# Attention and two MLPs on one core: weight conversions in every second item of attention instead of every third, and the combined tokens' last step in two pieces

## The chip, the core and the metric

The kernel runs on one core of a Trainium2 chip. A core has a matrix engine (PE, with its weight loads listed apart as PEld), a vector engine (DVE), an activation engine (ACT), a general engine (POOL) and a queue engine (SP), and DMA engines that move data. Each engine works through its own list of instructions in order, and waits on semaphores for the others. The metric is the device time of one execution in microseconds (us); a smaller number is better.

## What is computed

The reference runs three blocks one after the other, in float32 outputs:

```python
x = attention(q, k, v, s)            # 2 batches, 8 heads, 576 positions, 64 per head; causal, with a decay bias
x = x.transpose(0, 2, 1, 3).reshape(1152, 512)
h = x @ w_in;  x = maximum(0.01 * h, h) @ w_out        # w_in 512 x 2048, w_out 2048 x 512
p = domain_probs / domain_probs.sum(-1)                # 1152 x 4
out = sum over e of p[:, e] * (maximum(x @ w1[e], 0) @ w2[e])   # 4 experts, 512 x 1024 x 512
```

The weights `w_in` and `w_out` arrive as 64-bit floats, and the chip turns them into 32-bit ones. Every matrix operand is used as a pair of a rounded value (hi) and the rest (lo), and a product is three matmuls: hi with hi, lo with hi, hi with lo.

## The kernel before

The 1152 tokens are cut into a first part of 512 (part 0) and a second of 640 (part 1, 2 x 320). The program has these stretches, in the order of the trace:

- **Attention for part 0** (to about 67 us), then **attention for part 1** (to about 200 us). An item is one tile of queries and one or two heads; eight units of five items make up part 1. In each item there are three places at which other work is woven in. Each item's own steps (scores, exponentials, transposes, values, a finish) are spread over the following items by `STEPS` (L781).
- **The first MLP on part 0** (`mlps(phases[0])`, called `main`) is woven into attention and goes on after it up to about 228 us. Its up products are `ps_u<-x,w`, its down products `ps_d<-ht,w` with 512 columns; ACT and DVE turn an up product into the pair `ht`, and DVE adds a down product to `y`.
- **The first MLP on part 1** (about 228 to 334 us), then **the four experts** (to the end). Up products here go over combined tokens and combined weights: 7 products in the place of 8 (`paired_up`, L392), `ps_u<-t,w`.

Weights of the first MLP come in 16 units of 128 x 1024 numbers. `supply()` (L139) converts them, one unit after the other. One unit is an ACT instruction (`raw<-r`), two TENSOR_SCALAR and two SCALAR_TENSOR_TENSOR on DVE (`raw<-raw`, `raw<-r,raw`), each followed by a `yield`; then `finished()` issues the store of the unit to memory (`w_f<-raw`, from ACT's queue) and the fetch of the next 64-bit unit but one (`r`, also ACT's queue). Where the unit is needed at once, `finished()` also splits it into its pair (`w<-raw` on ACT, `w<-raw,w` on DVE). Otherwise `late_splits()` (L118) loads it back from `w_f` over SP's queue once its store was issued, and splits it in two halves of 512. At most four split units are held ahead (`WB`), and four `raw` buffers (`RAW`) are shared by all of these.

After attention, `first_sevens()` (L213) loads the first two weights of the MLP on part 1 from `w_f` and combines them: POOL makes the sums (`sums<-raw`), ACT rounds (`w<-raw`, `w<-sums`), POOL subtracts (`w<-sums,w`). At the same time `paired_steps()` (L364) combines the tokens of part 1, for two halves k of the 512 features: DVE makes four sums (`sums<-x`), then ACT rounds (`t<-x`, `t<-sums`) and DVE subtracts (`t<-x,t`, `t<-sums,t`). It is called again for part 0 and part 1 before the experts, then from `y`.

The order of instructions on each engine is the order of the program to the end of the first MLP on part 0 (`fixed = True`); from L898 a scheduler chooses it, and only the DVE subtractions of `paired_steps` stay in their order among those kept. In the attention loop for part 1 (L866 to L875) `at_ % 3` is the place in the item (0, 1, 2) and `i` the item: `main` gets places 0 and 1, `late_splits` places 0 and 2, and `supply` places 0 and 2 and place 1 of every third item. After attention (L885 to L893) `main` goes on, and every second step of it takes a step of one of the others. When attention closes (L876, L881) its memory and its accumulator banks are given up, and new pools are opened over them.

Of the kernel before, what the change touches and what calls it, by code (L numbers as in the profile page):

```python
# [19 lines left out]
def attention_moe_moe2(ctx: ExitStack, tc: tile.TileContext, q, k, v, s, w_in, w_out, probs, w1, w2, out):  # L20
# [54 lines left out]
    def f32(ap):  # L75
        return ap.bitcast(F32)
# [287 lines left out]
    def paired_steps(s, of, pool):  # L364

        n = half[s]
        t = t7[s] = pool.tile([P, 2, 7, 2, n], F32R, tag=f"t7_{s}", name=f"t7_{s}")
        for k in range(2):
            b11, b12 = of[:, k, :n], of[:, k, n:]
            b21, b22 = of[:, 2 + k, :n], of[:, 2 + k, n:]  # L370
            sums = scratch.tile([P, 4 * 320], F32, tag="scratch", name="sums")[:, : 4 * n].rearrange("p (s t) -> p s t", s=4)
            def subtract(*args):
                tc.keep_in_program_order(nc.vector.tensor_tensor(*args, ALU.subtract))

            subtract(sums[:, 1], b12, b11)
            subtract(sums[:, 2], b22, sums[:, 1])
            yield
            subtract(sums[:, 3], b22, b12)
            subtract(sums[:, 0], b21, sums[:, 2])
            yield  # L380
            for i, j, x in ((0, 2, of[:, k::2, :n]), (2, 3, of[:, 2 + k : 3 + k, n:]), (3, 7, sums)):
                hi, lo = (t[:, l, i:j, k] for l in range(2))
                nc.scalar.copy(hi, x)
                subtract(lo, x, f32(hi))
                yield
# [179 lines left out]
    def idling(n):  # L565

        for _ in range(n):
            nc.tensor.matmul(nothing[:, :P], idle[:, :P], idle[:, :P], start=True, stop=True)
# [209 lines left out]
    ending = False  # L778
# [4 lines left out]
    def attention():  # L783

        nonlocal ending
        items, starts, n = [], {}, 0
        i, split = 0, iter(())
        while n < units or i < len(items) + 8:
            if n < units and i == len(items):
                u = Unit(n)  # L790
                starts[n] = i
                items += [(u, *of) for of in u.items]
                if n + 2 < units and not 0 <= n + 2 - 2 * NP < 2:
                    load_keys(n + 2)
                    if n + 2 < 2 * NP:
                        decay(n + 2, k_e[(n + 2) % 3])
                if n in (2 * NP - 4, 2 * NP - 2):
                    load_keys(n + 4 if n == 2 * NP - 4 else n + 3)
                n += 1
            if n < units - 1 and i == starts[n - 1] + 2:  # L800
                load_values(n + 1)
            if i == starts[n - 1] and 2 * NP <= n < units:
                split = split_keys(n)
            for step, lag in STEPS:
                if 0 <= i - lag < len(items):
                    u, *of = items[i - lag]
                    step(u, *of)
                if lag == 1:
                    next(split, None)
                if lag in (1, 3, 7):  # L810

                    late = i - 5 + (lag == 7)
                    ending = lag != 3 and 0 <= late < len(items) and items[late][1:] == items[late][0].items[-1]
                    yield i
            i += 1
# [9 lines left out]
    with ExitStack() as phase:  # L825
        x_t[0] = phase.enter_context(tc.tile_pool(name="x0pool", bufs=1)).tile([P, 2, KD, sizes[0]], F32R, name="x0")
        wpool = phase.enter_context(tc.tile_pool(name="wpool", bufs=4))
        r64p = phase.enter_context(tc.tile_pool(name="r64p", bufs=2))

        OPENED = (24, 25, 26, 27, 28, 29, 31, 33, 35)  # L830

        CONVERTING = (*range(5, 16), *range(17, 31, 2))
        side, units_of_w, late, opened = attention(), supply(), late_splits(), 0
        nothing = ps_mm.tile([P, 512], F32, tag="mm", name="nothing")
        with tc.tile_pool(name="early", bufs=1) as early:
            ones = pads(early)
            sums = cumulative()
            next(sums)
            main = mlps(phases[0])

            for at_ in range(3 * 64):
                i = next(side)
                if done == 2 * NP and at_ % 3 == 2:
                    break
                if at_ % 3 == 0 and i in (6, 8):
                    nc.scalar.copy(q_s[i // 2 - 3][D:DK, 1, :, :QC], ones[D:DK])
                if at_ % 3 == 1:
                    if i < 18:
                        idling(2 if i < 6 else 1)
                    elif opened < len(OPENED) and i >= OPENED[opened] and opened < 3 * (done // 2):  # L850
                        next(main)
                        opened += 1
                if at_ % 3 < 2 and i >= 31:
                    onto_held()
                if at_ % 3 == 2:
                    if i == 3:
                        fetch64(1)
                    if i in (3, 4, 5):
                        next(sums)
                    if i in CONVERTING or i >= 31:  # L860
                        next(units_of_w)
        hidden_pool(phase, 6)
        heading = False

        owed = 0
        for at_, i in enumerate(side):  # L866
            if at_ % 3 < 2:
                owed += WOVEN * KD / (2.0 * (40 - 6))
                while owed >= 1.0:
                    next(main)  # L870
                    owed -= 1.0
            if at_ % 3 != 1:
                next(late, None)
            if (at_ % 3 != 1 or i % 3 == 0) and not ending:
                next(units_of_w, None)  # L875
        attn.close()  # L876
        w7pool = ctx.enter_context(tc.tile_pool(name="w7pool", bufs=2, side="right"))
        scratch = ctx.enter_context(tc.tile_pool(name="scratch", bufs=2, side="right"))
        t7pool = ctx.enter_context(tc.tile_pool(name="t7pool", bufs=1, side="right"))
        tokens = paired_steps(1, x_t[1], t7pool)  # L880
        banks.close()  # L881
        ps_mm = ctx.enter_context(tc.tile_pool(name="ps_all", bufs=8, space=PSUM))

        sevens = first_sevens()
        for m, _ in enumerate(main):  # L885
            if m % 2 == 0:
                next(late, None)
            if m % 4 == 0:
                next(tokens, None)
            if m % 4 == 2:  # L890
                next(units_of_w, None)
            if m % 4 % 2 and m >= 4:
                next(sevens, None)  # L893
        for _ in sevens:
            pass
        for _ in tokens:
            pass
# [57 lines left out]
```

## Time and profile before

| | us |
|---|---|
| median of 3 executions | 720.54 (717.39 to 970.85) |
| the profiled execution | 717.48 |
| its span, first to last instruction | 715.70 |

Share of the span in which an engine was busy: PE 97%, PEld 88%, DVE 61%, ACT 44%, POOL 35%. The granted clock of PE has a mean of 0.998 of full speed. A busy share is an average over stretches of different kind, and matmuls are pipelined with modelled ends; so the rows to read are those of a stretch, with the idle time in square brackets ahead of an instruction and, behind the arrow, what ended that idle time.

### The profile page before, as it was taken

Reading aid. Unit: us, or ns where it says so; the run is one execution under the profiler, and the core shown is the slowest. Engines: PE = TensorE matmul, PEld = TensorE weight load, DVE = VectorE, ACT = ScalarE, POOL = GpSimd, SP = SyncE. Lnnn points to the kernel's source line nnn. Section 1 sums busy time; section 2 is a strip of 40 time slices with the busy share of each in tenths; the row PEclk is TensorE's granted clock in tenths of the full one; section 3 lists DMA queues with packets and bytes.
Section 4 is the critical chain, followed back from the end, with each engine's and each line's share of the span. In section 5 each row is a group of like instructions: output and inputs, shape, how many; then the busy total and the mean of one; then the engine's idle time right before and its main releaser. Section 6 shows DMA issues by size and latency. Waiting matters only on the chain.

```text
span 715.7 us, 11167 instructions
## 1 busy us (share of the span) xinstructions
PE 696.9 (97%) x4256; PEld 633.2 (88%) x4256; DVE 433.7 (61%) x867; ACT 315.1 (44%) x640; POOL 253.9 (35%) x232
## 2 busy tenths in 40 slices
PE   8899999999988999999999999999999999999998
PEld 8778888888877999999988989889899898898986
DVE  7778788897767657735943634435435454364452
ACT  5757977875644574624422413323223142141210
POOL 6000000000039787964382522804526137142200
PEclk9999999999999999999999999999999999999999
DMA  9877688746442321320211211102011011010002
GB/s 232 207 195 208 194 211 245 220 143 235 177 177 61 118 82 66 119 60 30 60 60 31 59 31 59 60 1 89 31 57 54 8 60 60 1 59 1 1 36 97
DMA packets 43124, 69.61 MB, mean 97 GB/s; under 512 B 5616, under 2 KB 24832, under 8 KB 43072
## 3 DMA queue, kind: packets, MB, share of 16 engines
q1 hardware_dynamic: 32544, 40.83, 20.0%
q10 hardware_dynamic: 9376, 25.73, 10.6%
q0 software_dynamic: 1152, 2.36, 1.9%
q8 instruction: 33, 0.54, 0.3%
q14 instruction: 19, 0.16, 0.1%
HBM read 58.06 MB, written 10.82 MB: 96 GB/s over the span
## 4 chain that ended last, share of the span: by engine, by line
PE 82%; DVE 7%; DMA 4%; ACT 2%; POOL 2%; issue 1%; SPq 0%; ACTq 0%; POOLq 0%; DVEq 0%
PE ps_d L43 39%; PE ps_u L43 34%; PE ps_o L43 4%; PE ps_sc L43 3%; PE ps_pt L43 2%; DVE raw L43 2%; DMA qe<-in_q_dram 1%; DVE t L43 1%; ACT w L43 1%; DVE z L43 1%; DMA vs<-in_v_dram 1%; DMA raw<-w_f 1%; DMA ke<-in_k_dram 1%; DVE w L43 1%; POOL sums L43 1%
## 5 line engine op out<-in xcount | busy, mean ns | idle before, releaser
L43 PE MATMUL ps_u<-t,w 128*128 128x320 f32 (+1 forms) x1680 | 236.5, 299 | 1.1 <-DVE t L43 1.1
L43 PEld LDWEIGHTS ps_u<-t,w 128*128 128x128 f32 x1680 | 233.0, 189 | 4.8 <-DVE t L43 1.4
L43 PE MATMUL ps_d<-w,ht 128*128 128x512 f32 (+1 forms) x876 | 203.4, 388 | 0.0
L43 PEld LDWEIGHTS ps_d<-w,ht 128*128 128x128 f32 x876 | 161.0, 188 | 31.5
L43 POOL TENSOR_TENSOR w<-raw,w 128x512 fp32r<-128x512 f32 (+2 forms) x72 | 108.0, 1522 | 218.9 <-ACT w L43 218.9
L43 ACT ACTIVATE ht<-ps_u 128x320 fp32r<-128x320 f32 (+2 forms) x176 | 74.4, 433 | 153.7 <-DVE ps_u L43 129.0
L43 PE MATMUL ps_d<-ht,w 128*128 128x320 f32 (+1 forms) x576 | 111.0, 343 | 4.7 <-DVE ht L43 2.8
L43 DVE SCALAR_TENSOR_TENSOR oacc<-ps_d,pn,oacc 128x512 f32<-128x512 f32 (+1 forms) x64 | 47.5, 742 | 104.0 <-PE ps_d L43 104.0
L43 ACT CAST w<-raw 128x512 fp32r<-128x512 f32 (+2 forms) x94 | 64.5, 722 | 87.4 <-PE ps_d L43 67.7
L43 PEld LDWEIGHTS ps_d<-ht,w 128*128 128x128 f32 x576 | 92.3, 190 | 12.0 <-DVE ht L43 3.2
L43 DVE SCALAR_TENSOR_TENSOR ht<-ps_u,ht 128x320 fp32r<-128x320 f32 (+1 forms) x128 | 56.3, 452 | 23.3 <-ACT ht L43 22.0
L43 DVE TENSOR_TENSOR ps_u<-ps_u,tmp 128x320 f32<-128x320 f32 (+1 forms) x120 | 56.2, 471 | 23.3 <-PE ps_u L43 21.7
L43 POOL TENSOR_TENSOR sums<-raw 128x256 f32<-128x256 f32 x48 | 38.4, 818 | 66.1 <-PE ps_d L43 64.6
L43 DVE TENSOR_TENSOR tmp<-ps_u,tmp 128x320 f32<-128x320 f32 (+1 forms) x80 | 36.8, 463 | 40.4 <-PE ps_u L43 39.4
L43 POOL TENSOR_TENSOR w<-sums,w 128x1024 fp32r<-128x1024 f32 x24 | 58.2, 2424 | 5.3 <-ACT w L43 5.3
L43 PEld LDWEIGHTS ps_o<-vs,pv 128*128 128x128 f32 x400 | 53.5, 191 | 6.8 <-issue 2.3
L43 PE MATMUL ps_u<-x,w 128*128 128x512 f32 x192 | 56.3, 410 | 0.9 <-DVE x L43 0.9
L43 PE MATMUL ps_o<-vs,pv 128*128 128x65 f32 (+1 forms) x400 | 53.3, 267 | 2.1 <-DVE xo L43 1.2
L43 POOL DMA_DIRECT2D kd<-in_k_dram x8 | 4.8, 603 | 127.3 <-PE ps_sc L43 67.0
L43 ACT ACTIVATE z<-z,mn 128x256 f32<-128x256 f32 (+4 forms) x72 | 42.4, 588 | 12.0 <-DVE mn L43 7.2
L43 DVE CUSTOM_DVE_ANT_0 z<-ps_sc,mask 128x256 f32<-128x256 f32 (+4 forms) x72 | 36.0, 501 | 12.5 <-PE ps_sc L43 9.7
L43 ACT COPY pv<-ps_pt 128x512 f32<-128x512 f32 (+3 forms) x80 | 33.2, 424 | 21.2 <-PE ps_pt L43 20.7
(78 smaller groups left out, 647.0 us busy)
## 6 DMA issues: line engine op xcount, KB each, us to landing
raw<-in_moe_w_dram SPq DMA_DIRECT2D x32, 512.0 KB
raw<-w_f SPq DMA_DIRECT2D x22, 512.0 KB
r<-in_moe_w_in_dram ACTq DMA_DIRECT2D x8, 1024.0 KB
w_f<-raw ACTq DMA_DIRECT2D x16, 512.0 KB
r<-in_moe_w_out_dram ACTq DMA_DIRECT2D x8, 1024.0 KB
kd<-in_k_dram POOLq DMA_DIRECT2D x8, 288.0 KB, 6.0
kr<-in_k_dram SPq DMA_DIRECT2D x8, 288.0 KB
vs<-in_v_dram SPq DMA_DIRECT2D x8, 256.0 KB
```

What stands on the lines that cost most here:

```text
L43: ins = call(*args, **kw)
```

## The change

Two lines are edited. In `paired_steps` the last step, over the four sums at once (slots 3 to 6 of the seven), is made in two pieces, of slots 3 and 4 and of slots 5 and 6; each has its ACT instruction, its DVE subtraction and its `yield`. In the attention loop for part 1, `supply` gets place 1 of every second item instead of every third.

```diff
@@ paired_steps
-            for i, j, x in ((0, 2, of[:, k::2, :n]), (2, 3, of[:, 2 + k : 3 + k, n:]), (3, 7, sums)):
+            for i, j, x in ((0, 2, of[:, k::2, :n]), (2, 3, of[:, 2 + k : 3 + k, n:]), (3, 5, sums[:, :2]), (5, 7, sums[:, 2:])):
                 hi, lo = (t[:, l, i:j, k] for l in range(2))
                 nc.scalar.copy(hi, x)
                 subtract(lo, x, f32(hi))
                 yield
@@ the attention loop
             if at_ % 3 != 1:
                 next(late, None)
-            if (at_ % 3 != 1 or i % 3 == 0) and not ending:
+            if (at_ % 3 != 1 or i % 2 == 0) and not ending:
                 next(units_of_w, None)
```

**DVE at the end of attention.** The names: `raw` is a unit under conversion (`raw_2285` is the last of the 16 before, `raw_2227` after), `xo` the last output of attention, `ht` a hidden tile, `w` a split weight, `y0` the sum of down products of part 0. Before:

```order
L43 TENSOR_TENSOR w_2294<-raw_2232,w_2294 128x512 x2
L43 TENSOR_SCALAR raw_2285<-raw_2285 128x1024
L43 TENSOR_SCALAR st_2319<-ps_o_2221 128x6
L43 RECIPROCAL st_2319<-st_2319 128x6
L43 TENSOR_TENSOR xo_2322<-ps_o_2221,st_2319 128x384
L43 TENSOR_SCALAR raw_2285<-raw_2285 128x1024
L43 TENSOR_TENSOR ht_2328<-ps_u_2300,ht_2328 128x512
L43 SCALAR_TENSOR_TENSOR raw_2285<-r64_2219,raw_2285 128x1024 x2
L43 TENSOR_TENSOR w_2341<-raw_2308,w_2341 128x512 x2
L43 TENSOR_TENSOR y0_1310<-ps_d_2333,y0_1310 128x512
```

The same place after the change:

```order
L43 SCALAR_TENSOR_TENSOR raw_2227<-r64_2136,raw_2227 128x1024 x2
L43 TENSOR_TENSOR ht_2308<-ps_u_2271,ht_2308 128x512
L43 TENSOR_TENSOR w_2312<-raw_2251,w_2312 128x512 x2
L43 TENSOR_SCALAR st_2335<-ps_o_2240 128x6
L43 RECIPROCAL st_2335<-st_2335 128x6
L43 TENSOR_TENSOR xo_2338<-ps_o_2240,st_2335 128x384
L43 TENSOR_TENSOR ht_2343<-ps_u_2319,ht_2343 128x512
L43 TENSOR_TENSOR w_2351<-raw_2317,w_2351 128x512 x2
L43 TENSOR_TENSOR y0_1317<-ps_d_2347,y0_1317 128x512
```

The four conversion instructions of the last unit no longer stand between `w`, `xo`, `ht` and `y0`: the last pair of them now stands ahead of the `ht` two places earlier, and the rest further up.

**DVE where the first combined tokens are made**, after attention (`t7_1` are the combined tokens of part 1, `sums` their sums for k = 0). Before:

```order
L43 TENSOR_TENSOR t7_1_2387<-x1_98,t7_1_2387 128x320
L43 TENSOR_TENSOR ht_2462<-ps_u_2437,ht_2462 128x512
L43 TENSOR_TENSOR t7_1_2387<-sums_2388,t7_1_2387 128x4x320
L43 TENSOR_TENSOR ht_2485<-ps_u_2466,ht_2485 128x512
L43 TENSOR_TENSOR sums_2496<-x1_98 128x320
```

After:

```order
L43 TENSOR_TENSOR t7_1_2399<-x1_98,t7_1_2399 128x320
L43 TENSOR_TENSOR ht_2474<-ps_u_2449,ht_2474 128x512
L43 TENSOR_TENSOR t7_1_2399<-sums_2400,t7_1_2399 128x2x320
L43 TENSOR_TENSOR ht_2497<-ps_u_2478,ht_2497 128x512
L43 TENSOR_TENSOR t7_1_2399<-sums_2400,t7_1_2399 128x2x320
L43 TENSOR_TENSOR y0_1317<-ps_d_2501,y0_1317 128x512
```

The second hidden tile (`ht_2485`, now `ht_2497`) stood behind all four slots and now stands between the two pieces. ACT's list has the same shape at this place: the second `ht` behind the first piece, the second piece behind the `ht`.

**SP's loads of stored weights**, over the whole program (each row 128 x 1024 numbers; other loads stand between the rows). Before, then after:

```order
L43 DMA raw<-w_f_73 128x1024
L43 DMA raw<-w_f_73 128x1024 x10
L43 DMA raw<-w_f_73 128x1024 x11
```

```order
L43 DMA raw<-w_f_73 128x1024
L43 DMA raw<-w_f_73 128x1024
L43 DMA raw<-w_f_73 128x1024
L43 DMA raw<-w_f_73 128x1024
L43 DMA raw<-w_f_73 128x1024 x10
L43 DMA raw<-w_f_73 128x1024 x11
```

There are 22 such loads before and 25 after; the three more are units that `late_splits` loads back, and they stand among the loads of attention's keys and values.

## Rows read from the trace of the kernel before

**Rows 1.** Waits of PE: waiting tile, releaser, us in total, times, longest.

```profile
PE ps_d L43 <- DVE ht L43: 2.8, 1, 2.8
PE ps_d L43 <- DVE y L43: 1.9, 1, 1.9
PE ps_u L43 <- DVE t L43: 1.1, 1, 1.1
```

**Rows 2.** Timeline of PE from 190 us: start, duration, instruction, count, [idle before].

```profile
196.21 3.68 PE L43 MATMUL ps_d<-ht,w 128*128 128x512 f32 x15
201.76 5.71 PE L43 MATMUL ps_d<-ht,w 128*128 128x512 f32 x24 [1.88 <-DVE y L43]
207.31 5.60 PE L43 MATMUL ps_u<-x,w 128*128 128x512 f32 x24
212.75 2.71 PE L43 MATMUL ps_d<-ht,w 128*128 128x512 f32 x11
218.25 10.29 PE L43 MATMUL ps_d<-ht,w 128*128 128x512 f32 x37 [2.79 <-DVE ht L43]
```

**Rows 3.** Windows: length, busy time by engine (count), PE's clock, DMA share, GB/s.

```profile
200.00:202.00 2.00, 0.24 (x1) 0.27 (x2) 1.97 (x6) 0.15 (x1) 0.00 (x0) 1.00 0.22 88
...
218.00:220.00 2.00, 1.75 (x4) 1.41 (x5) 1.97 (x4) 0.00 (x0) 1.92 (x3) 0.59 0.08 2
220.00:222.00 2.00, 2.00 (x6) 1.53 (x5) 1.58 (x4) 0.84 (x1) 2.00 (x3) 0.55 0.05 5
```

**Rows 4.** Timeline of DVE around the end of attention.

```profile
195.81 2.48 DVE L43 SCALAR_TENSOR_TENSOR raw<-r,raw 128x1024 uint32<-128x1024 uint32 x2
...
200.93 0.68 DVE L43 TENSOR_TENSOR y<-ps_d,y 128x512 f32<-128x512 f32 x1
...
207.51 0.69 DVE L43 TENSOR_TENSOR y<-ps_d,y 128x512 f32<-128x512 f32 x1 [1.24 <-PE ps_d L43]
...
214.23 3.37 DVE L43 TENSOR_TENSOR t<-sums,t 128x1280 fp32r<-128x1280 f32 x1 [2.15 <-ACT t L43]
217.52 0.68 DVE L43 TENSOR_TENSOR ht<-ps_u,ht 128x512 fp32r<-128x512 f32 x1
```

**Rows 5.** Timeline of ACT in the same stretch.

```profile
199.42 0.73 ACT L43 CAST t<-x 128x640 fp32r<-128x640 f32 x1
...
210.77 0.59 ACT L43 ACTIVATE ps_u<-ps_u 128x512 f32<-128x512 f32 x1
211.98 1.05 ACT L43 CAST w<-sums 128x1024 fp32r<-128x1024 f32 x1 [0.62 <-POOL sums L43]
212.94 1.26 ACT L43 CAST t<-sums 128x1280 fp32r<-128x1280 f32 x1
214.10 0.58 ACT L43 ACTIVATE ht<-ps_u 128x512 fp32r<-128x512 f32 x1
```

**Rows 6.** Timelines of POOL and of SP's queue in that stretch.

```profile
213.86 2.39 POOL L43 TENSOR_TENSOR w<-sums,w 128x1024 fp32r<-128x1024 f32 x1
...
201.08 1.74 SPq L43 DMA_DIRECT2D raw<-w_f  x4
```

**Rows 7.** Window over attention for part 1, columns as in rows 3.

```profile
60.00:200.00 140.00, 137.83 (x875) 120.89 (x873) 117.60 (x220) 102.00 (x188) 3.49 (x6) 1.00 0.66 197
```

**Rows 8.** DVE by line, 60 to 200 us: count | busy us, mean ns.

```profile
L43 DVE SCALAR_TENSOR_TENSOR raw<-r,raw 128x1024 uint32<-128x1024 uint32 x26 | 31.7, 1219 | 0.4
L43 DVE TENSOR_SCALAR raw<-raw 128x1024 f32<-128x1024 f32 (+1 forms) x26 | 17.9, 689 | 0.3
```

**Rows 9.** Timeline of DVE and POOL ahead of the experts.

```profile
338.12 1.48 DVE L43 TENSOR_TENSOR t<-sums,t 128x1280 fp32r<-128x1280 f32 x1
...
345.91 3.38 DVE L43 TENSOR_TENSOR t<-sums,t 128x1280 fp32r<-128x1280 f32 x1
...
345.54 6.02 POOL L43 TENSOR_TENSOR w<-raw,w 128x1024 fp32r<-128x1024 f32 x2 [15.26 <-ACT w L43]
```

**Rows 10.** DVE by shape, 335 to 352 us: count | busy us, mean ns.

```profile
L43 DVE TENSOR_TENSOR t<-y,t 128x640 fp32r<-128x640 f32 x2 | 1.6, 816 | 0.0
```

## Prediction

> **What bounds the kernel now.** The busy shares and the waits of PE come first. PE is busy 97% of the span (the table of the profile above), and nearly all that it waits for is in three lines: a hidden tile `ht` 2.8 us, a sum `y` 1.9 us and combined tokens `t` 1.1 us, once each [rows 1]. So the change can gain only at these three places, or lose by making PE wait where it does not now. The timeline of PE tells where the first two are: both just after attention, at 201.76 and 218.25 [rows 2]. The 24 products from 201.76 to 207.31 take 5.55 us, 0.231 us each; this pace gives what each place really costs, since a busy matmul's end is modelled.
>
> - First gap: 15 products from 196.21 would be over at 196.21 + 15 x 0.231 = 199.68; the next starts at 201.76 [rows 2]. Lost 2.08 us.
> - Second gap: 11 products from 212.75 end at 215.29; the next starts at 218.25 [rows 2]. Lost 2.96 us.
> - [...] The 37 products from 218.25 last 10.29 us less about 0.16 of overhang (5.71 - 5.55), that is 10.13; at the pace they need 8.55 [rows 2]. Lost 1.58 us.
>
> These are 6.62 us in all. In attention itself PE idles 140.00 - 137.83 = 2.17 us while DVE is busy 117.60 of 140.00 [rows 7]: PE sets the time there, and DVE, at 84%, is close behind.
>
> **Why the two gaps are there.** At the first, PE starts the first product in the reopened accumulators, and is released by the sum `y` that DVE begins at 200.93 [rows 4], over a second after its products were done. DVE was late: the last unit's two bit operations hold it from 195.81 for 2.48 us, and what follows in its list is late in turn [rows 4]. At the second, PE needs the rest of the hidden tile, made at 217.52. DVE had it behind the subtraction over four slots, 3.37 us from 214.23, which began when ACT's rounding of those slots (212.94, 1.26 us) was done; that in turn stood behind `w<-sums` at 211.98, which waited for POOL's sums [rows 4, 5]. POOL's sums wait for a load that SP issues at 201.08 with three others [rows 6], behind the store of the last unit.
>
> **The supply in every second item.** Attention for part 1 covers about 40 items, so place 1 comes some 20 times instead of 13: seven steps more, a little over one unit of six. The order agrees: the last unit's instructions leave the end of attention for a place two hidden tiles earlier.
>
> First gap. With the 2.48 us gone, and two TENSOR_SCALAR ahead of it, DVE is free when the last products are done. `y` then starts as at 207.51, 0.04 us behind the end of its products (201.76 + 5.71 = 207.47) [rows 2, 4], so at 196.21 + 3.68 + 0.04 = 199.93. It lasts 0.68, to 200.61; PE starts 0.15 later, as before (201.76 against 200.93 + 0.68), at 200.76. **Gain 1.00 us.** Bounds: 0 if another instruction is late there, 1.00 if none, since PE must wait for this sum anyway.
>
> Second gap, upstream. The last store no longer waits for bit operations that end at 198.3, so the loads queued behind it on SP and POOL's sums come earlier too, and ACT's `w<-sums` need not wait for POOL. This alone moves ACT only by the 0.62 us of its idle time [rows 5]; it counts together with the pieces, below.
>
> Cost in attention. One more unit lies there: two SCALAR_TENSOR_TENSOR of 1.219 us and two TENSOR_SCALAR of 0.689 us [rows 8], 3.82 us, and its split in two 512-wide subtractions, by the 0.68 us of the 512-wide `y` [rows 4] 1.36 us: 5.2 us of DVE in the 22.4 us that it is idle [rows 7]. DVE works in order; behind an inserted operation wait reads of scores and sums, and PE for these. Nothing if the idle time takes them, 5.2 us if all lies on the path. A gain cannot be ruled out: the units stand more evenly now, and at most the 2.17 us of idle time is to be had. PE loses 2.17 us while DVE is 84% busy; in proportion, 5.2 us more on 117.6 would cost 0.1 us, but waits grow faster than load when an engine fills up, so I take **0.5 us**.
>
> The three more loads of 0.5 MB, from 22 to 25, add 1.5 MB to 197 GB/s over 140 us (27.6 MB), at a DMA share of 0.66 [rows 7]. They stand on SP ahead of loads of keys and values, and each waits for its store; the loads behind them come some us later, but are wanted a unit or two later (17 us a unit: 140 us over some eight units). Nothing, and if a unit came too late, a few us once. A late split is in two halves of 512 and so costs an instruction more on ACT and DVE, 3 times, some tenths of a us off the path.
>
> **The last step in two pieces.** At the second gap the hidden tile now stands behind the first piece only, on ACT and DVE. All PE times move up by the 1.00 of the first gap. ACT: the second write of the first hidden tile starts at 210.77 - 1.00 = 209.77 and ends 0.59 later, at 210.36; `w<-sums` takes 1.05, to 211.41; the first piece, as wide as the 0.73 us row at 199.42, ends at about 212.1 [rows 5]. The second tile's products are over at 207.31 + 5.60 - 1.00 = 211.9, so ACT makes its `ht` from 212.1 (0.58) and the second write behind it (0.59), to 213.3. DVE: the first piece from 212.1. Its cost is not in the trace; the 640-wide subtraction alone is 0.816 us [rows 10], half of the 3.37 is 1.69 us [rows 4]. POOL works at this place (2.39 us from 213.86) [rows 6], and it will have its rounding done about as early as DVE, so I take 1.69: to 213.8. The rest of `ht` takes 0.68, to 214.5, and PE follows 0.05 later (217.52 + 0.68 against 218.25). PE wants it at 215.29 - 1.00 = 214.29. Lost about 0.2 to 0.4 where 2.96 were: **gain 2.55 us**. Bounds: 2.96; and 0.69 if ACT and DVE keep their old times, only 1.69 us is saved and PE waits 1.00 longer.
>
> Here the trace shows four slots at 1.48 us while POOL is idle and at 3.38 us while POOL works [rows 9]. [...] At 0.82 us a piece `ht` would start at 213.3, the gap would be gone and the sum 0.4 us lower.
>
> The clock. With a gap of 0.4 us, far under the 2.08 us behind which the clock stayed up, it should not fall: **gain 1.58 us**; 0 if it falls all the same.
>
> The other calls: for the other half of these tokens, and ahead of the experts, the order puts the two pieces next to each other or where DVE has room. Ahead of the experts DVE is full and PE waits 1.1 us for the last step [rows 1]. Two pieces of 0.816 are 0.15 us more than 1.48 [rows 9, 10], twice here: **cost 0.3 us**. Bounds: a gain of 1.1 if PE can go on after the first piece, a loss of 1.0 if the later start meets more of POOL's 6.02 us [rows 9].
>
> **Sum**, against the profiled execution: 717.48 - 1.00 - 2.55 - 1.58 + 0.5 + 0.3 = 713.15, say **713.2 us**. That execution is 0.09 above the lowest and 3.06 below the median of the three runs; I predict a run like it.
>
> **Rivals.**
> - *DVE becomes the bound in attention.* In its list the added work stands ahead of score reads. For: 84% busy. Against: PE now waits only 2.17 us there. If half of 5.2 lands, 713.15 - 0.5 + 2.6 = 715.3; if all, 717.9, slower than before. It passes 717.48 from 4.8 us on.
> - *The wait goes over to POOL and ACT.* POOL's work comes earlier and meets the first piece, ACT's list stays as long, the gap stays above 2 us and the clock falls: 713.15 + (2.55 - 0.69) + 1.58 = 716.6. For: 3.37 against 1.48. Against: ACT has idle time at this place.
> - *The pieces do nothing* (a change that isn't what it says): true in the calls where they stand side by side, not at the second gap, where the order puts `ht` between them. It would be the case above without the 0.69: 717.3.
> - *More is won:* the more even supply ends waits in attention, and PE goes on after the first piece ahead of the experts: 713.15 - 0.5 - 1.5 - 0.3 - 0.8 = 710.1.
>
> **Chances.** My forecast (711.3 to 715) 0.60; DVE in attention 0.15, of which 0.05 slower than before; POOL and ACT 0.13; pieces without effect 0.03; more won 0.09. The range that leaves out no more than 2 in 10: 709.8 to 717.3; the forecast's own is 711.3 to 715. All cases lie within 2% of either figure of before, about what a measurement of this kernel can tell from no change; the best of them is 1.5% under the median of before. Faster by over 2%: 0.03; within: 0.94; slower: 0.03, for a wait that no row shows.
>
> **What would show it.** In the timeline of PE the first gap 1.1 us instead of 2.08 and the second under 0.5; full clock from 200 to 230 us; `y` at 0.04 us behind its products; DVE's first piece at 0.8 to 1.7 us with `ht` behind it; attention's PE idle time of 2.17 us grown by no more than 1 us; the last wait ahead of the experts 1 to 1.5 us. I am wrong if attention ends over 2 us later, if the second gap stays above 2 us, or if the clock falls behind a short one.

## The result and the profile after

The change makes the kernel slightly slower: 723.24 us, the median of 15 executions (720.43 to 726.43), against 718.82 us before (15 executions, of which one of 970.85 us is left out of the ratio). The ratio is 1.0053, with a 95% interval of 1.0035 to 1.0071, so about 2.5 to 5 us are lost. The prediction was 713.2 us with a range of 709.8 to 717.3: wrong in its size and in its direction. The profiled execution took 721.17 us with a span of 719.4, and its granted clock is 0.993 of full speed (0.998 before).

The waits of PE, in the view of [rows 1]: the two waits that the prediction wanted gone are short (`y` 0.9 us, `ht` 0.7), but the wait for combined tokens `t` went from one of 1.1 us to three of 4.2 in all, and the wait for score reads (`mn`) from one of 0.3 us to three of 3.0. The first four rows are of the changed kernel, the last is of the kernel before.

```profile
PE ps_u L43 <- DVE t L43: 4.2, 3, 1.6
PE ps_sc L43 <- DVE mn L43: 3.0, 3, 1.3
PE ps_d L43 <- DVE y L43: 0.9, 1, 0.9
PE ps_d L43 <- DVE ht L43: 0.7, 1, 0.7
PE ps_sc L43 <- DVE mn L43: 0.3, 1, 0.3
```

The timeline of PE behind attention, to be laid beside [rows 2]: both gaps are about a microsecond, and the 37 products behind the second take 8.69 us where they took 10.29. The clock no longer falls here (1.00 from 218 to 224 us).

```profile
199.62 3.68 PE L43 MATMUL ps_d<-ht,w 128*128 128x512 f32 x15
204.18 5.69 PE L43 MATMUL ps_d<-ht,w 128*128 128x512 f32 x24 [0.88 <-DVE y L43]
209.71 5.60 PE L43 MATMUL ps_u<-x,w 128*128 128x512 f32 x24
215.15 2.65 PE L43 MATMUL ps_d<-ht,w 128*128 128x512 f32 x11
218.54 8.69 PE L43 MATMUL ps_d<-ht,w 128*128 128x512 f32 x37 [0.74 <-DVE ht L43]
```

The stretch of attention as a whole, in the view of [rows 7] (PE, PEld, DVE, ACT and POOL busy, clock, DMA share, GB/s), hardly shows what happened: PE is busy 136.69 us instead of 137.83, and DVE 117.90 instead of 117.60, although it does a unit more in the stretch.

```profile
60.00:200.00 140.00, 136.69 (x864) 120.12 (x863) 117.90 (x223) 101.25 (x189) 3.61 (x6) 0.99 0.72 216
```

**A finer measure.** PE makes the same 4256 products in both kernels. For each product I take its start in one trace less its start in the trace of before; where this difference grows, time is lost. The table gives the growth by stretch, in us (stretches by the times of before), for the changed kernel and for the experiments below, whose names are told there. It is worked out from the starts in the traces, one execution each, and read at the last product that starts ahead of the time named. A lower clock of PE is in these figures as well as its waits. e5, e7, e9, e10 and e11 were executed once each, so they are read by this table and not by their times.

| kernel | to 66 | attention, 66 to 196 | first gap, to 217 | second gap, to 226 | to 262 | to 345 | experts' start, to 360 |
|---|---|---|---|---|---|---|---|
| forecast | 0 | +0.5 | -1.0 | -4.1 | 0 | 0 | +0.3 |
| **changed kernel** | +0.4 | **+3.0** | -1.1 | -3.7 | +1.4 | +0.2 | **+3.6** |
| supply alone (e1) | +1.3 | +1.9 | -1.1 | -3.0 | +1.1 | +0.2 | +0.1 |
| pieces alone (e2) | -0.2 | +0.7 | -0.1 | -3.3 | +1.4 | +0.3 | +3.7 |
| supply, one piece split (e3) | -0.9 | +4.7 | -1.1 | -3.7 | +1.6 | +0.1 | 0.0 |
| other places (e4) | +0.8 | +4.0 | -1.1 | -3.7 | +1.4 | +0.3 | +3.9 |
| before, POOL in halves (e5) | +2.7 | -0.1 | -0.1 | -1.9 | +1.5 | +0.7 | -1.1 |
| late places (e6) | -1.1 | +0.5 | -1.1 | -3.0 | +1.2 | +0.2 | 0.0 |
| late, one piece split (e7) | +3.0 | -0.1 | -1.1 | -3.7 | +1.6 | +0.2 | 0.0 |
| late, split, halves (e8) | +4.0 | +0.3 | -1.1 | -3.7 | +1.9 | +0.8 | -1.1 |
| early places (e9) | +0.2 | +3.1 | -1.1 | -3.0 | +1.1 | +0.2 | 0.0 |
| before again (e10) | +2.0 | +0.4 | +1.9 | -2.9 | +1.1 | +0.3 | 0.0 |
| pieces and halves (e11) | +2.8 | -0.1 | +1.8 | -3.5 | +1.8 | +1.0 | +0.1 |

Behind 360 us every row stays where it is. So the gains came nearly as forecast, and were more than lost in attention, at the start of the MLP on part 1, and ahead of the experts.

### The profile page after: what moved, and what is told of

It is laid out like the page before. It is cut to its first block, busy times and chain, and to the rows that moved or that the text cites. A ratio compares the mean times of both kernels' runs of the same rounds, so it can differ in the third digit from the quotient of the medians.

```text
span 719.4 us, 11183 instructions
## 1 busy us (share of the span) xinstructions
PE 700.1 (97%) x4256; PEld 636.6 (88%) x4256; DVE 444.3 (62%) x876; ACT 316.1 (44%) x649; POOL 253.6 (35%) x232
## 4 chain that ended last, share of the span: by engine, by line
PE 76%; DVE 8%; DMA 2%; ACT 1%; issue 1%; DVEq 0%; SPq 0%; ACTq 0%
PE ps_d L43 39%; PE ps_u L43 32%; PE ps_o L43 2%; DVE t L43 2%; DVE raw L43 1%; PE ps_sc L43 1%; PE ps_pt L43 1%; DMA raw<-w_f 1%; DVE sums L43 1%; DVE z L43 1%; ACT w L43 1%; DVE w L43 1%; DVE ks L43 1%; DVE y L43 1%; DMA w_f<-raw 0%
## 5 line engine op out<-in xcount | busy, mean ns | idle before, releaser
L43 POOL TENSOR_TENSOR w<-raw,w 128x512 fp32r<-128x512 f32 (+2 forms) x72 | 109.6, 1542 | 225.8 <-ACT w L43 225.8
L43 ACT CAST w<-raw 128x256 fp32r<-128x256 f32 (+2 forms) x97 | 64.8, 703 | 85.3 <-PE ps_d L43 74.3
L43 POOL TENSOR_TENSOR sums<-raw 128x256 f32<-128x256 f32 x48 | 36.6, 783 | 56.1 <-DMA raw<-w_f 54.7
L43 ACT ACTIVATE z<-z,mn 128x256 f32<-128x256 f32 (+4 forms) x72 | 42.3, 587 | 12.5 <-DVE mn L43 10.5
```

What stands on the lines that cost most here:

```text
L43: ins = call(*args, **kw)
```

## The loss ahead of the experts: two pieces, two turns

Here PE waits twice, at 349.09 and 352.00, where it waited once. DVE, POOL and PE of the changed kernel from 345.5 us, in two views each (the first ends ahead of the second piece, so that its row is of one instruction alone):

```profile
346.33 2.71 DVE L43 TENSOR_TENSOR t<-sums,t 128x640 fp32r<-128x640 f32 x1
345.96 5.31 POOL L43 TENSOR_TENSOR w<-raw,w 128x1024 fp32r<-128x1024 f32 x2 [15.34 <-ACT w L43]
346.33 5.62 DVE L43 TENSOR_TENSOR t<-sums,t 128x640 fp32r<-128x640 f32 x2
348.31 2.95 POOL L43 TENSOR_TENSOR w<-raw,w 128x1024 fp32r<-128x1024 f32 x1
349.09 1.29 PE L43 MATMUL ps_u<-t,w 128*128 128x320 f32 x7 [1.44 <-DVE t L43]
352.00 6.58 PE L43 MATMUL ps_u<-t,w 128*128 128x320 f32 x32 [1.63 <-DVE t L43]
```

The two pieces take 5.62 us; the whole step took 3.38 in the kernel before [rows 9]. Read the ends: POOL's first instruction ends at about 348.35 (the second starts at 348.31), and DVE's first piece ends 0.7 us later (346.33 + 2.71 = 349.04). POOL's second ends at 345.96 + 5.31 = 351.27, and DVE's second piece 0.7 us later (346.33 + 5.62 = 351.95). A 640-wide subtraction alone takes 0.816 us [rows 10]. So each piece looks as if it waited until POOL's instruction was over and then ran at its own pace. The whole step of before fits: POOL's first instruction would end about 2.4 us behind 345.54, at 347.95, and 1.35 later DVE is done, at 349.29 (345.91 + 3.38).

That is a reading of two traces. Two experiments test it against the account in the prediction, where a piece is simply half as long as the whole.

**POOL in halves (e5)**: the kernel before, with POOL's subtraction in two instructions.

```diff
     def split_steps(raw, shape):
         ...
-        (nc.vector if fixed else nc.gpsimd).tensor_tensor(w[:, 1], raw, f32(w[:, 0]), ALU.subtract)
+        if fixed:
+            nc.vector.tensor_tensor(w[:, 1], raw, f32(w[:, 0]), ALU.subtract)
+        else:
+            for part in (slice(0, 512), slice(512, 1024)):
+                nc.gpsimd.tensor_tensor(w[:, 1, part], raw[:, part], f32(w[:, 0, part]), ALU.subtract)
```

> The kernel before, with one edit: in the stretches behind the first MLP on part 0, where POOL makes the subtraction of a split weight, it makes it in two instructions of 512 columns instead of one of 1024. Ahead of the experts two of these stand beside DVE's subtraction over four slots (3.38 us from 345.91 in the kernel before, where the first of POOL's ends at 347.94). Theory A, an instruction of the one engine waits until the instruction of the other that is under way is over, and only then runs at its own 1.35 to 1.48 us: DVE's four slots end 1.0 to 1.4 us earlier, in 2.0 to 2.5 us instead of 3.38, and PE's wait of 1.15 us there shrinks to under 0.3. Theory B, the two engines share a rate, so each instruction is slower by what the other moves meanwhile: POOL moves the same numbers, DVE still needs 3.2 to 3.6 us and PE still waits about 1.1 us.

Measured, DVE, POOL (three views, the later ones begin inside the first) and PE:

```profile
348.74 2.28 DVE L43 TENSOR_TENSOR t<-sums,t 128x1280 fp32r<-128x1280 f32 x1
348.37 1.30 POOL L43 TENSOR_TENSOR w<-raw,w 128x512 fp32r<-128x512 f32 x1 [15.25 <-ACT w L43]
348.37 3.80 POOL L43 TENSOR_TENSOR w<-raw,w 128x512 fp32r<-128x512 f32 x2 [15.25 <-ACT w L43]
339.79 16.62 PE L43 MATMUL ps_u<-t,w 128*128 128x256 f32 x119
```

DVE's whole step takes 2.28 us instead of 3.38: it ends 1.35 us behind the first half of POOL (348.37 + 1.30 = 349.67, and 348.74 + 2.28 = 351.02). POOL's second half in turn ends at 348.37 + 3.80 = 352.17, 1.15 us behind DVE, close to the 1.30 of the first half. PE runs 119 products from 339.79 with no wait; the stretch gains 1.1 us. The 2.28 us lie in the 2.0 to 2.5 of theory A and not in the 3.2 to 3.6 of theory B. In these rows the two engines take turns, instruction by instruction, and the one that waits loses what is left of the other's instruction: DVE 0.93 us (348.74 to 349.67), and POOL 1.39 (349.63 to 351.02). In e8, which has the same edit, the step takes 2.28 us again.

**Pieces and halves (e11)**: the edit of e5 and the two pieces, with the supply of before.

> The supply as before, the step in two pieces in all calls, and POOL's subtraction in halves of 512 in the later stretches. Theory, each piece of DVE waits for the one instruction of POOL that is under way (1.3 us as a half, 2.4 us whole) and then runs at its own 0.7 to 0.8 us: ahead of the experts the two pieces end after 3 to 4 us instead of 5.6, and of the 3.4 us lost there by the pieces alone 1.5 us or less is left. Rival, they share a rate: the two pieces together need 5 us or more, and the loss stays above 2.5 us.

DVE and PE (the first row's view ends inside the second piece's time):

```profile
349.67 3.44 DVE L43 TENSOR_TENSOR t<-sums,t 128x640 fp32r<-128x640 f32 x2
351.33 1.29 PE L43 MATMUL ps_u<-t,w 128*128 128x320 f32 x7 [0.34 <-DVE t L43]
353.16 5.34 PE L43 MATMUL ps_u<-t,w 128*128 128x320 f32 x32 [0.54 <-DVE t L43]
```

Two pieces beside halves take 3.44 us instead of 5.62, and the two waits of PE are 0.34 and 0.54 instead of 1.44 and 1.63. The loss of the stretch falls from 3.6 us to 0.1; against the halves without pieces (-1.1) the pieces still cost 1.2. As the theory expected, 3.44 us lies in its 3 to 4 and not in the 5 or more of its rival. Not all of the 3.6 us is waiting. The two waits of the changed kernel, 3.07 us, stand against one of 1.1 before, some 1.9 more; the other 1.6 or so is the clock, which fell behind the second wait there (0.51 from 352 to 354 us) and, behind the same wait, in e2 (0.50 from 351 to 353 us) and in e4 (0.50 from 355 to 357 us), and held in e11 behind 0.54 us (1.00 from 354 to 356 us).

The rows of the two pieces agree: a piece ends 0.7 us behind the instruction of POOL that it met, whether that one had 2.0 us left (346.33) or 2.3 (the second piece). An estimate by turns, two instructions of POOL at the 2.4 us of [rows 6] and the 0.7 us of these rows behind the second, gives 5.5 us of DVE ahead of the experts for the two pieces, where the forecast added 0.3 us to what the step took before (3.38 us).

The group of all such subtractions, by form (busy us, mean ns of one), before and then after. What was 12.5 us of DVE in six instructions is 20.9 in twelve, for the same numbers:

```profile
L43 DVE TENSOR_TENSOR t<-sums,t 128x1280 fp32r<-128x1280 f32 x4 | 9.9, 2480 | 2.1 <-ACT t L43 2.1
L43 DVE TENSOR_TENSOR t<-sums,t 128x1024 fp32r<-128x1024 f32 x2 | 2.6, 1287 | 0.0
```

```profile
L43 DVE TENSOR_TENSOR t<-sums,t 128x640 fp32r<-128x640 f32 x8 | 14.8, 1878 | 0.9 <-ACT t L43 0.9
L43 DVE TENSOR_TENSOR t<-sums,t 128x512 fp32r<-128x512 f32 x4 | 6.1, 1529 | 0.0
```

## The two parts apart

**Supply alone (e1)** and **pieces alone (e2)** each undo one part of the change. Against the changed kernel, first e1, then e2:

```diff
-(3, 5, sums[:, :2]), (5, 7, sums[:, 2:])
+(3, 7, sums)
```

```diff
-(at_ % 3 != 1 or i % 2 == 0)
+(at_ % 3 != 1 or i % 3 == 0)
```

> The conversions of weights in every second item of attention, and the combined tokens' last step whole, in one piece, as before. Theory (from the two traces, product by product): attention loses 3.0 us with this supply, the first gap behind it gains 1.0, the second gap gains up to 1 us by the earlier loads but stays near 2 us, and the two later places (about 234 us and ahead of the experts) stay as before the change: 1 to 2.5 us slower than before, and 2 to 3 us faster than the change. Rival (my working in the prediction): attention costs 0.5 us only, and this part alone gains about 0.5 us.

> The supply in every third item as before, and the last step of the combined tokens in two pieces in all calls. Theory: nothing changes in attention; the second gap behind it gains 2.5 to 4 us; at about 234 us a new wait of PE of 1.3 us stands, and ahead of the experts 3.5 us more are lost than before: 0 to 2 us slower than before. Rival (the prediction): the pieces cost 0.3 us ahead of the experts and nothing at 234 us, so this part alone gains 3 to 4 us.

The supply alone: 717.70 us, ratio 1.0003 (0.9976 to 1.0030), no difference to before. The pieces alone: 721.53 us, ratio 1.0045 (1.0021 to 1.0069), slower. So nearly all of the change's loss comes with the pieces. My theory for the supply alone, 1 to 2.5 us lost, is not borne out, though the interval (1.7 us gained to 2.2 lost) leaves room for its lower half. The table tells why. The second gap gains 3.0 us with the supply alone, and 3.3 with the pieces alone, while both together gain 3.7. They take the same wait away; the pieces add 0.7 us to what the supply does. In each of these figures 1.58 us is the clock, which fell behind this gap in the first trace of before alone [rows 3]. The wait itself was 2.79 us there [rows 2], and is 1.41 with the supply (e1), 1.05 with the pieces (e2) and 0.74 with both. The program of before up to here waits 2.41 us in a second execution (e5), where the clock held (1.00 from 218 to 224 us) and 1.9 us are gained with no edit at this place. Rows of e1, e2 and e5:

```profile
219.01 8.73 PE L43 MATMUL ps_d<-ht,w 128*128 128x512 f32 x37 [1.41 <-DVE ht L43]
216.97 8.69 PE L43 MATMUL ps_d<-ht,w 128*128 128x512 f32 x37 [1.05 <-DVE ht L43]
220.45 8.73 PE L43 MATMUL ps_d<-ht,w 128*128 128x512 f32 x37 [2.41 <-DVE ht L43]
```

**One piece split (e3)**: the supply of the change, and the two pieces only for the first half of the features of part 1, right behind attention.

```diff
-(3, 5, sums[:, :2]), (5, 7, sums[:, 2:])
+*(((3, 5, sums[:, :2]), (5, 7, sums[:, 2:])) if fixed and k == 0 else ((3, 7, sums),))
```

> The supply of the change, and the step in two pieces in one place alone: the first half of the features of part 1, right behind attention. Everywhere else it is one piece. Theory: the new wait at 234 us (1.3 us) and the loss ahead of the experts (3.5 us) are gone, the second gap stays short and attention still costs 3.0 us: 1 to 2.5 us faster than before, 4.5 to 6 us faster than the change. Rival (the loss ahead of the experts comes from the supply, or from chance between two executions): within 1.5 us of the change.

718.15 us, ratio 1.0003 (0.9975 to 1.0031). The loss ahead of the experts is gone (0.0 in the table), so it belongs to the pieces there. But the kernel is not faster than before as I expected: 1.6 us are lost between 226 and 262 us all the same (below), and attention in its trace lost 4.7 us.

## The loss in attention: earlier conversions

In the changed kernel PE waits at three fixed places for a score read. The first, in DVE's list: the split of a weight (`w<-raw,w`) now stands ahead of the score read `z` at 77.20. In the kernel before, `z` came straight behind `ht` (its row is the last but one), and the split (the last row) followed 2.4 us later. PE and DVE of the changed kernel, then DVE of the kernel before:

```profile
77.82 0.33 PE L43 MATMUL ps_sc<-ks,qs 128*128 128x128 f32 x1 [0.95 <-DVE mn L43]
95.88 0.37 PE L43 MATMUL ps_sc<-ks,qs 128*128 128x128 f32 x1 [1.31 <-DVE mn L43]
166.95 0.33 PE L43 MATMUL ps_sc<-ks,qs 128*128 128x128 f32 x1 [0.69 <-DVE mn L43]
75.11 0.69 DVE L43 TENSOR_TENSOR ht<-ps_u,ht 128x512 fp32r<-128x512 f32 x1 [1.98 <-ACT ps_u L43]
76.06 1.23 DVE L43 TENSOR_TENSOR w<-raw,w 128x1024 fp32r<-128x1024 f32 x1 [0.27 <-ACT w L43]
77.20 0.55 DVE L43 CUSTOM_DVE_ANT_0 z<-ps_sc,mask 128x384 f32<-128x384 f32 x1
```

```profile
75.28 0.55 DVE L43 CUSTOM_DVE_ANT_0 z<-ps_sc,mask 128x384 f32<-128x384 f32 x1
77.67 1.22 DVE L43 TENSOR_TENSOR w<-raw,w 128x1024 fp32r<-128x1024 f32 x1
```

These three waits, 0.95, 1.30 to 1.66 and 0.61 to 0.89 us, stand at the same products in e1, e3 and e9; in the kernels whose first thirty items are as before the first and the third are not there and the second is 0.3 us. Product by product they cost 1.1, 1.0 and 0.9 us in the changed kernel, and about 2 us come back at other places, where the kernel before lost more. Behind the second wait the clock fell in the changed kernel (0.51 from 96 to 98 us and 0.64 from 98 to 100); by an estimate from these windows that is about 1.6 of the 3.0 us. In e1, where it held (1.00 from 60 to 200 us), attention costs 1.9. Three experiments vary the places.

**Other places (e4)**: both parts of the change, with place 1 in five other items of every ten.

```diff
-(at_ % 3 != 1 or i % 2 == 0)
+(at_ % 3 != 1 or i % 10 in (1, 3, 6, 7, 8))
```

> Both parts of the change, but the third place is given in other items: again five of every ten, items 1, 3, 6, 7 and 8 of a ten instead of the even ones, so never in the first item of a unit, behind whose conversions the score read stands for which PE waits in the changed kernel. Theory that the place costs and not the amount: attention loses under 1 us instead of 3.0, and the kernel is 2 to 3 us faster than the change. Rival, the amount costs (one more unit on an engine that is 84% busy): within 1 us of the change.

722.89 us, ratio 1.0067 (1.0041 to 1.0092), like the change; attention costs 4.0 us. My theory, that only the first item of a unit is a bad place, falls; its rival, that the amount costs, is not refuted by this run. The first wait is gone, and another has come in its stead: the same split of a weight now stands ahead of `xo`, which reads accumulators of attention (`ps_o`). The profile names no releaser for this wait of PE (`issue`); that it is `xo` is read from its end at 80.69, 0.1 us ahead of PE's start. PE, then DVE:

```profile
80.79 1.36 PE L43 MATMUL ps_o<-vs,pv 128*128 128x130 f32 x10 [1.28 <-issue]
78.57 1.23 DVE L43 TENSOR_TENSOR w<-raw,w 128x1024 fp32r<-128x1024 f32 x1 [0.92 <-ACT w L43]
80.13 0.56 DVE L43 TENSOR_TENSOR xo<-ps_o,st 128x384 f32<-128x384 f32 x1
```

**Late places (e6)** and **early places (e9)** cut the change of the supply in two, with the step in one piece. Against the kernel before, first e6, then e9:

```diff
-(at_ % 3 != 1 or i % 3 == 0)
+(at_ % 3 != 1 or i % 3 == 0 or i >= 70)
```

```diff
-(at_ % 3 != 1 or i % 3 == 0)
+(at_ % 3 != 1 or (i % 2 == 0 if i < 70 else i % 3 == 0))
```

> The kernel before with one edit: supply gets place 1 of every third item as before, and in addition of every item from 70 on, the last ten of attention, so the last unit still leaves the end of attention but the first thirty items are as before. The step of the combined tokens is one piece. Theory A, attention's cost came from the earlier items (three places in the trace of the change) and from fetches that the faster supply overtakes: product by product against the trace of before, attention costs under 1 us, the first gap gains 1.0, the second 2.5 to 3.5; 2.5 to 4 us faster than before. Theory B, the last unit has to be made in the same attention anyway and costs wherever it stands: attention costs 2 to 3 us and the kernel is within 1.5 us of before.

> The counterpart of the late places: supply gets place 1 of every second item up to item 69 and of every third from item 70 on; the step is one piece. Theory, the conversions that come earlier in the first thirty items put score reads off, and so cost: product by product against the trace of before, attention costs 1.5 to 3.5 us, the first gap gains 1.0 and the second about 3.0. Rival, attention's cost lay in the last ten items or was chance between executions: attention costs under 0.8 us, as with the late places.

The late places cost 0.5 us in attention and still gain 1.1 and 3.0 at the two gaps; the kernel takes 715.74 us, ratio 0.9972 (0.9950 to 0.9994), faster than before. The early places cost 3.1, of which 1.4 is a wait at 146.23 us behind a load (of the kind told below). That settles where the loss is: in the first thirty items. The three waits show how it comes about, by what stands ahead of a read that PE waits for. That DVE's load has no part in it is not shown: in the last ten items DVE has more room too, in the kernel before 23.44 of 31 us busy (76%) against 84.64 of 98 (86%) in about the first thirty. Before, columns as in [rows 7]:

```profile
67.00:165.00 98.00, 96.29 (x612) 84.49 (x612) 84.64 (x159) 75.99 (x137) 2.90 (x5) 1.00 0.69 197
165.00:196.00 31.00, 30.65 (x192) 26.63 (x191) 23.44 (x44) 19.23 (x37) 0.00 (x0) 1.00 0.60 215
```

Part of the loss is not at fixed places. In e3 ACT stood before a fetch of 64-bit weights and before a reload, and PE waited for ACT's copies (`pv`) behind them. ACT, then PE:

```profile
124.53 1.14 ACT L43 ACTIVATE raw<-r 128x1024 f32<-128x1024 f32 x1 [2.08 <-DMA r<-in_moe_w_in_dram]
135.90 1.14 ACT L43 CAST w<-raw 128x512 fp32r<-128x512 f32 x2 [2.27 <-DMA raw<-w_f]
127.85 0.66 PE L43 MATMUL ps_pt<-ident,z 128*128 128x128 f32 x4 [1.49 <-ACT pv L43]
140.76 0.55 PE L43 MATMUL ps_pt<-ident,z 128*128 128x128 f32 x3 [1.46 <-ACT pv L43]
```

These two waits, 2.95 us, are about what e3's 4.7 us have over the 1.9 of e1, whose attention is the same program. In e9 ACT waits 1.83 us for such a fetch and PE 1.65 us for `pv` behind it, at 146.23. ACT waits for such loads with the old supply too (5.7 us in all in before again), there without a loss for PE; whether the earlier conversions make it likelier, the runs don't tell.

**Before again (e10)**: an unchanged copy, for the spread between two executions.

> The kernel before, unchanged, for a second trace of it. Theory, what differs between two executions of one program lies in the stretch of loads up to 60 us (up to some 4 us either way) and at places where a load is waited for; from 60 us to the end of attention the two traces stay within 1 us, and the two gaps, and the wait ahead of the experts, are within 0.3 us. Rival, attention itself varies by 2 to 3 us from execution to execution, and the cost read from the trace of the change is chance.

Attention is 0.4 us from the first trace, so a cost there with the changed supply is not chance: the kernels with the old or late supply lie between -0.1 and 0.7, those with earlier conversions between 1.9 and 4.7. Its size does vary, with the clock (3.0 in the changed kernel) and with the loads (4.7 in e3), against 1.9 in e1. The stretch to 66 us varies by 5 us over all rows, with nothing changed there. And, against my expectation, the first gap lost 1.9 us: there the clock fell, as it had behind the second gap in the first trace [rows 3]. Windows (the clock is the third figure from the end) of before again, then of e5, whose program is that of before up to here:

```profile
204.00:206.00 2.00, 1.42 (x3) 1.16 (x4) 1.23 (x3) 0.00 (x0) 0.00 (x0) 0.58 0.60 135
206.00:208.00 2.00, 2.00 (x7) 1.57 (x6) 0.00 (x0) 0.00 (x0) 0.00 (x0) 0.56 0.97 383
```

```profile
204.00:206.00 2.00, 1.61 (x7) 1.38 (x8) 1.04 (x3) 0.00 (x0) 0.00 (x0) 1.00 0.63 176
220.00:222.00 2.00, 1.55 (x7) 1.27 (x8) 1.97 (x4) 0.00 (x0) 1.92 (x3) 1.00 0.10 3
```

So of three executions of this stretch, the clock fell behind the second gap in one, behind the first in one, and behind neither in one. e2 and e11 run the same program up to the second gap: behind the first gap the clock held in e2 (1.00 from 202 to 204 us) and fell in e11 (0.51 from 206 to 208 us). In the changed kernel, e1, e3 and e4 it held behind both gaps (1.00 from 200 to 240 us); e6 to e9, which have more supply too, gain as much at both in the table as these.

## What the second gap gave back, and the best version

From 226 to 262 us the changed kernel loses 1.4 us, but so do all others, 1.1 to 1.9, the kernel before again too (1.1); only the first trace of before did not. With the pieces and whole instructions of POOL it is a wait for `t` at 234 us: two pieces, 4.31 us where the whole took 1.69, beside POOL. Without them PE goes on there and waits later for a load, as in e1, where ACT stands before it. PE and DVE of the changed kernel, then ACT and PE of e1:

```profile
234.06 6.86 PE L43 MATMUL ps_u<-t,w 128*128 128x320 f32 x45 [1.12 <-DVE t L43]
229.70 4.31 DVE L43 TENSOR_TENSOR t<-sums,t 128x640 fp32r<-128x640 f32 x2
```

```profile
239.87 1.05 ACT L43 CAST w<-raw 128x1024 fp32r<-128x1024 f32 x1 [1.54 <-DMA raw<-w_f]
241.30 5.98 PE L43 MATMUL ps_d<-ht,w 128*128 128x320 f32 x39 [0.80 <-ACT ht L43]
```

The load goes into a buffer that POOL must have read (POOL's subtractions start at 231.60 in e1 and at 229.75 in the first trace of before); that it is this wait for POOL which delays it was not tried.

**Late, one piece split (e7)** is e6 with the split of e3; **late, split, halves (e8)** adds POOL's halves of e5.

> The kernel with the third place in the last ten items, and the step in two pieces for the first half of the features behind attention alone. Theory, the two parts take the same wait away and only 0.4 to 0.7 us of the second gap is left for the pieces: up to 0.7 us faster than with the late places alone. Rival (the prediction's account, which gave the pieces 2.55 us and the clock's 1.58): 3 us faster than with the late places alone.

> All three: the third place in the last ten items, two pieces for the first half of the features behind attention alone, and POOL's subtraction in halves of 512 in the later stretches. Theory: 1.0 from the first gap, 3.0 to 3.7 from the second, 1.0 to 1.3 ahead of the experts, less up to 1 us in attention: 4 to 6 us faster than before. Rival, one instruction of POOL stands in the other's way for as long in two halves, and attention costs 2 to 3 us: 1 to 2.5 us faster than before.

At the second gap e7 gains 3.7 us, 0.7 more than e6: the theory, not the prediction's account. But 0.4 of it goes again by 262 us. e8 took 716.59 us, ratio 0.9969 (0.9950 to 0.9989): faster than before by about 2.2 us (0.3% of 719), less than the 4 to 6 that I expected. Counted behind 66 us, its trace stands at -2.8 us against the first trace of before and -3.6 against before again. My sum had left out what is lost again from 226 to 345 us. e6 and e8 can't be told apart by their times; both beat the kernel before and the changed one.

## Why the prediction was wrong, point by point

- **What PE waits for**: "nearly all" in three lines was too much. The three of [rows 1] are 5.8 of some 15 us in that view; waits of 2.6 us in all for ACT's copies `pv`, in attention, are among the rest.
- **First gap, -1.00**: right, -1.07 in every kernel with the earlier last unit. `y` begins 0.04 us behind the end of its products (203.34 against 199.62 + 3.68), and PE goes on at 204.18, 0.15 us behind `y`.
- **Second gap, -2.55, and the clock, -1.58**: together -4.13 forecast, -3.65 measured. Without the clock's 1.58 the gap gained 2.07. The size was nearly right, the account half wrong. I let the pieces carry it and gave the supply only ACT's 0.62 us; e1 gains 2.95 without a piece, 1.37 of it without the clock. The pieces' own part beside the supply is 0.7 us. And the clock's 1.58 was a property of one trace: of three executions of this program one had it at this gap, one at the other. Against the three the two gaps together gain about 3.7 us (-4.72, against 0, -1.0 and -2.0), not 4.7; that the sum came near is in part luck.
- **A piece at 1.69 us**, half of 3.37: the step that failed. I read the 3.37 us beside POOL as a slower rate, so that half of the numbers take half of the time; that was an estimate, and no run shows a piece at 1.69. The first piece behind attention took 2.50 us, until POOL's `w<-sums` was over and 0.7 us more (rows of DVE and POOL below); the second, which began as POOL's next instruction ended, took 0.81. In these rows the price of a piece is what is left of POOL's instruction plus 0.7 us.
- **Experts' handover, +0.3, bounds to +1.0**: +3.6. The same step. I counted "two pieces of 0.816" for POOL idle and one meeting with POOL at most; the two pieces met two instructions of POOL, 5.62 us for 3.38, so PE waited some 1.9 us longer, and behind the second wait the clock fell, for the other 1.6 (0.51 from 352 to 354 us, in the last fence of this section). Rows 9 and the ends of POOL's instructions would have told it: 3.38 us is the rest of one POOL instruction and 1.35.
- **Attention, +0.5, bounds -2.2 to +5.2**: +3.0, inside the bounds, wrong in the value. The step that failed is "nothing if the idle time takes them": 22 us of idle time did not help where an instruction stood in front of a read that PE was waiting for (0.95, 1.31 and 0.69 us). The busy share of 84% over the whole stretch did not show that; the order of the rows did. That waits grow faster than load, from which I took the 0.5, was an estimate that no run shows. The three places cost 1.9 us net in e1; the changed kernel's 3.0 holds about 1.6 us of a lower clock besides, which no term of the sum had. Of the rivals, "DVE becomes the bound" came nearest: it has the added work ahead of score reads. Places are shown; load and place were not told apart.
- **Three more reloads, 0**: neither right nor wrong by the runs. In e3 PE lost some 3 us behind a fetch and a reload; in the changed kernel's own trace it lost nothing to them.
- **The call for the other half of the features** was costed at nothing, with "DVE has room". It cost a new wait of 1.12 us at 234, though most of that is lost there without the pieces too.
- **Range**: its upper end, 717.3, is that of the case in which the pieces do nothing. A loss of 1.0 ahead of the experts and of 2.6 to 5.2 in attention were bounds that were never added up. Attention's 3.0 and the experts' 3.6 both lay beyond my value, the second beyond its bound too, and nothing in the cases let both happen. Of the 10.0 us from 713.2 to 723.24 some 8 lie in the traced executions (4.3 us gained in the forecast, 3.7 lost in time); the other 2 are the traced execution's distance to the median.

The first piece and what POOL did beside it:

```profile
215.38 2.50 DVE L43 TENSOR_TENSOR t<-sums,t 128x640 fp32r<-128x640 f32 x1 [0.90 <-ACT t L43]
214.80 2.40 POOL L43 TENSOR_TENSOR w<-sums,w 128x1024 fp32r<-128x1024 f32 x1 [3.63 <-ACT w L43]
```

The clock in the changed kernel, in attention behind the wait at 95.88 and ahead of the experts:

```profile
96.00:98.00 2.00, 2.00 (x7) 1.69 (x8) 1.16 (x3) 1.54 (x3) 0.00 (x0) 0.51 0.98 278
352.00:354.00 2.00, 2.00 (x7) 1.83 (x8) 2.00 (x7) 0.71 (x2) 0.00 (x0) 0.51 0.83 159
```

## What to carry to other kernels

Before a subtraction of DVE like these is cut in pieces, look at what POOL does beside it: here two pieces took 5.62 us beside two instructions of POOL where the whole took 3.38, and 2.28 with POOL's instruction in halves, so try POOL's instructions first. Work put into an engine's idle time can cost by what stands behind it in its list, so look up the next read that the bounding engine waits for, and put the work where that read comes first; here the last ten items cost at most 0.5 us and the first thirty 1.9 and more, though the last ten also have more idle time. When two edits aim at one wait, count its gain once.

## What the runs showed of the hardware that was not expected

- In these subtractions DVE and POOL took turns by whole instructions: DVE's 640-wide one, 0.816 us alone [rows 10], took 2.50, 2.71 and about 3.0 us beside POOL, ending each time 0.7 us behind POOL's instruction. In these rows the wait lies inside the instruction's duration and not in the idle time ahead of it (2.71 us at 346.33, with no idle time in its row).
- The clock fell behind a wait of PE of 1.31 us in the changed kernel (95.88) and not behind 1.66 us at the same product in e1, whose mean clock is 1.00; behind gaps of over 2 us it fell in the first trace of before (2.79), in e10 (2.33) and in e11 (2.10), and held in e5 (2.41). Its cost can't be booked to a gap from one trace.
- The first 66 us, with their loads, differ by up to 5 us between traces in which nothing was changed there. Differences of a few tenths of a per cent are better read product by product, behind that stretch.
